# Key groups 4 to 7 transposed by DMA instead of by TensorE, with loads and transposes of the neighbouring turns moved, in a fused attention and MLP kernel

## The chip, the cores and the metric

The kernel runs on one core of a Trainium2 chip. The metric is the device time of one launch in microseconds. Three runs of the kernel before took 818.16, 818.71 and 819.41 us; the median, 818.71 us, is the time to compare with. Besides these there is one profiled execution, whose trace is read below.

## The reference, cut to what matters

```python
xn = layernorm(x)                                  # x: 2048 tokens x 576, bf16
# A: attention over the last 512 cached positions; 32 query heads, 16 key groups, head size 128
q = (xn @ wq).reshape(B, Sq, 32, 128).transpose(0, 2, 1, 3)
k = repeat(k_cache[:, :, Sk - 512:, :], 2, axis=1)
v = repeat(v_cache[:, :, Sk - 512:, :], 2, axis=1)
s = (softmax(q @ k.T * 128 ** -0.5) @ v).reshape(B, Sq, 4096) @ wo
# B: a token mixer (two 576x576 products with shifts by +-1 and +-2 tokens between), then an MLP of 4608
h = gelu(layernorm(xn) @ w1)
x1 = xn + shifted(h) @ w2
b = x1 + gelu(layernorm(x1) @ w3) @ w4
out = x + s * silu(b)
```

## The kernel before, in words

The 2048 tokens are worked in 4 query blocks of 512 (`QB`). The attention walks 128 **turns** `u`, one for each block and head (`u = 32*block + head`; in the code `Hq = 32`). In turn `u` TensorE computes the scores of head `u` (`stage_s`, L545: four 128x512 products with the transposed keys `kT`), the query projection of head `u+1` (`stage_q`, L526), and the value products of head `u-1` (`stage_v`, L564). ScalarE takes the exponentials (L549). VectorE copies the queries and divides by the row sums. The order is written out by hand for SP, POOL and PE in the loop at the end of the attention: for each turn the table `fill` gives side work that is put behind the first score products, `pe_fill` gives extra products for TensorE, and `turn` gives transposes that SP issues at the turn's end. The Tile scheduler orders VectorE and ScalarE.

Side work that the change touches:

- **Keys.** `load_k(i)` (L356) brings key groups 4i to 4i+3 into a staging tile of `stage_pool`, which has two buffers under one name. Loads 0 and 1 are issued by SP at the start, loads 2 and 3 by POOL in turns 4 and 12. Groups 0 to 3 are transposed by TensorE before turn 0. Groups 4 to 7 (`prep_k`, L372) are transposed by TensorE in turns 5, 7, 9 and 11, four 128x128 products each, into a PSUM tile that VectorE copies to `kT` (L376). Groups 8 to 15 are transposed by DMA (`tr_k`, L381), issued by SP in turns 9 to 12 and 17 to 20. Group g is first read in turn 2g.
- **Head outputs.** `stage_t(v)` (L577) transposes the output of head `v` by DMA from an `o` tile (18 buffers) into an `oT` tile (36 buffers). SP issues one per turn, none in the turns that have a `tr_k`, and two per turn after turn 37 until the backlog is gone.
- **Weights.** POOL loads `wq` for four heads in every fourth turn (`load_wq`, L339 and L346, two buffers): turns 3, 7, 11 and so on; load j is first read by `stage_q` in turn 4j-1, four turns after its issue. POOL loads `wo` in eight pieces of four heads (L412), in turns 9, 13, ... 37. Each waits with a small copy (L243) until that turn's exponentials are there. Values (L362) are loaded in turns 3 to 20, the next block's `x` (L332) in turn 14.
- **First output projection.** The product of block 0's heads with `wo` (`wo_groups`, L269) stands in turns 43 to 47 (`WO0 = 43`).
- **Mixer transposes.** `ln2_apply` (L209) and `tr2` (L260) normalise blocks 0 and 1 for the mixer and transpose them by DMA in turns 34 to 37 and 42 to 45 into two tiles of `stage_pool`, which is read only after the attention.
- **Mixer.** After the attention `b1_rest(b)` ends with a gelu on ScalarE (L847) and a DMA transpose (L848); the pairs (`b1_pair`, L812) have two gelus each. The list `aside` puts `b1_rest(3)` into step 3, ahead of the gelus of the pair of step 2.

SP and POOL are in-order queues: what waits holds up everything behind it.

Of the kernel before, what the change touches and what calls it, by code (L numbers as in the profile page):

```python
# [8 lines left out]
P = 128  # L9
ACT = mybir.ActivationFunctionType  # L10
ALU = mybir.AluOpType
AX = mybir.AxisListType
BF16 = mybir.dt.bfloat16
# [18 lines left out]
def kernel(  # L32
# [14 lines left out]
    nc = tc.nc  # L47
# [4 lines left out]
    _, Hkv, Sk, Dh = A_k_cache.shape  # L52
    assert Dh == P
    Hq = A_wq.shape[1] // Dh
# [7 lines left out]
    QB = 512  # L62
    NB = S // QB
    TB = QB // P
# [3 lines left out]
    NDC = NF + 1  # L68
    DP = NDC * P
    DCH = [(i * P, min(P, D - i * P)) for i in range(NDC)]  # L70
    M0 = 512
    R0 = D - M0
# [4 lines left out]
    OFF = 16  # L77
# [150 lines left out]
    oT_pool = octx.enter_context(tc.tile_pool(name="oT_pool", bufs=OT, side="right"))  # L228
    fence_pool = ctx.enter_context(tc.tile_pool(name="fence", bufs=2))
    tctx = ctx.enter_context(ExitStack())  # L230
    stage_pool = tctx.enter_context(tc.tile_pool(name="stage_pool", bufs=2))
    so_pool = tctx.enter_context(tc.tile_pool(name="so_pool", bufs=1))
    so_t, oT_t, xnnT = {}, {}, {}
    w1_all = xT_b[0][:].rearrange("p k q -> p (k q)")
# [16 lines left out]
                                in_=w1_tail.rearrange("p (j two s) -> p j two s", two=2, s=c4)[:, :, half, 0:P])  # L251
    flag_m = [None]

    def stage():
        return stage_pool.tile([P, DP * TB], BF16, name="stage")

    def tr2(b, tt, home=None):
        if tt == 0:
            xnnT[b] = (home or stage())[:].rearrange("p (k t) -> p k t", k=NDC)
        nc.sync.dma_start(out=xnnT[b][:, :, tt * P:(tt + 1) * P], in_=xm_b[b % 2][:, tt, :], transpose=True)  # L260

    FLAG_OPS = (ALU.max, ALU.min)
# [36 lines left out]
    with ExitStack() as actx:  # L299
# [5 lines left out]
        kT = res.tile([P, Hkv, W], BF16, name="kT")  # L305
        v_sb = res.tile([P, Hkv, KCH, VW], BF16, name="v_sb")
        NWQ = 2
        KDMA = 8
        PLAIN = 4
        wq_b = [res.tile([P, NDC, 4 * Dh], BF16, name=f"wq_b{i}") for i in range(NWQ)]  # L310
        ri_b = res.tile([P, Hq, TB], FP32, name="ri_b")
# [38 lines left out]
        kst_t = {}  # L350

        def load_k(i, eng=None, step=4):
            kst_t[i] = stage()
            dst = kst_t[i][:, 0:4 * W].rearrange("p (g a) -> p g a", g=4)
            for g in range(0, 4, step):
                (eng or nc.gpsimd).dma_start(  # L356
                    out=dst[:, g:g + step, :],
                    in_=A_k_cache[0, 4 * i + g:4 * i + g + step, K0:, :].rearrange("g (p kc) d -> p g (kc d)", p=P))
# [30 lines left out]
        for tt in range(TB):  # L389
            if tt:  # L390
                (nc.sync if tt < TB - 1 else nc.scalar).dma_start(out=x_first[:, tt, :],
                                                                  in_=x2[tt * P:(tt + 1) * P, :])
# [4 lines left out]
        with tc.manual_schedule(engines={SP}):  # L397
            load_k(0, nc.sync, 2)
            for m0 in (0, 2 * Dh):
                cols = slice(m0, m0 + 2 * Dh)  # L400
                nc.sync.dma_start(out=wq_b[0][:, 0:NF, cols],
                                  in_=A_wq[0:NF * P, cols].rearrange("(kc p) m -> p kc m", p=P))
# [220 lines left out]
            return PLAIN - 1 <= u < U - 1 and u % 4 == 3  # L623

        ln2_at = (7, Hq + 3, 2 * Hq - 4, 2 * Hq + 20)
        tr2_at = (Hq + 2, Hq + 10, 3 * Hq - 10, 3 * Hq - 5)
        WO0 = Hq + 11
        tr_k_at = {u: g for u, g in zip([*range(9, 13), *range(17, 21)], range(KDMA, Hkv))}
        x_at = (14, Hq + 12, 2 * Hq + 4)
        ln1_at = (19, Hq + 21, 2 * Hq + 16)  # L630

        for b in range(1, NB):
# [37 lines left out]
                pe_late.append((2 * g - 3, g))  # L670
        for j in range(2, NB * 8):
            at(4 * (j - 1) - 1, lambda j=j: load_wq(j))
        for i, u in enumerate((9, 13, 17, 21, 25, 29, 33, 37)):
            at(u, lambda i=i, u=u: late(pT_t[u][0][0:1, 0:1], lambda: load_wo(i)))
        for b in range(NB):
            at((b + 1) * Hq + 1, lambda b=b: row_range(b))
# [33 lines left out]
        for u in range(1, U + 1):  # L710
            n = 1
            if u in tr_k_at:
                turn[u] = [lambda g=tr_k_at[u]: tr_k(g)]
                n = 0
            elif u > Hq + 5:
                n = 2
            if u < WO0 + TB + 1:
                n = min(n, OT - done)
            for _ in range(min(n, u - done)):
                turn.setdefault(u, []).append(lambda v=done: stage_t(v))  # L720
                done += 1
# [28 lines left out]
    with ExitStack() as bctx:  # L750
# [23 lines left out]
        hq = mres.tile([P, HW], BF16, name="hq")  # L774
        hs = mres.tile([P, S], BF16, name="hs")
        h4 = [mres.tile([P, TB, P], BF16, name=f"h4_{i}") for i in range(NB)]
# [61 lines left out]
        def b1_rest(b):  # L838
            def ops(half, tt, k):
                w = w1_m[half, k, :].rearrange("p (g s) -> p g s", g=4)[:, :, P:c4] if k < NF else w1_q[half, :, :]  # L840
                return xnnT[b][half, k, tt * P:(tt + 1) * P], w

            pr = small_products(ops)
            gs = gs_pool.tile([P, TB, R0], FP32, name="gs")
            nc.vector.tensor_copy(out=gs[:], in_=pr[0])
            nc.vector.tensor_tensor(out=gs[:], in0=gs[:], in1=pr[1], op=ALU.add)
            nc.scalar.activation(out=h4[b][:, :, 0:R0], in_=gs[:], func=ACT.Gelu_apprx_tanh)  # L847
            nc.sync.dma_start(out=hq[:, OFF + b * QB:OFF + (b + 1) * QB].rearrange("p (t q) -> p t q", t=TB),  # L848
                              in_=h4[b][:].rearrange("p t c -> p (t c)"), transpose=True)

        def shifts(b):
            for g in (1, 0, 3, 2):
# [36 lines left out]
        with tc.manual_schedule(engines={SP, POOL, PE, DVE, ACTE}):  # L889
            for b in range(2, NB):  # L890
                home = mres.tile([P, DP * TB], BF16, name=f"xnnT{b}")
                for tt in range(TB):
                    tr2(b, tt, home)
            e = small.tile([P, 1], FP32, name="nr_e")
            nc.scalar.activation(out=e[:], in_=so_t[NB - 1][:, 1, 0:1], func=ACT.Gelu_apprx_tanh)
            for half in range(2):
                nc.gpsimd.dma_start(out=w1_q[HALVES[half], :, :],
                                    in_=w1_tail.rearrange("p (g s) -> p g s", g=4)[:, :, P:c4])
            for half in range(2):
                for g in range(4):  # L900
                    p0 = half * DR + g * rsz
                    nc.gpsimd.dma_start(out=w2_q[p0:p0 + rsz, :], in_=w2_by_g[g, P:c4, :])
            for t in (hb[:, :, OFF - PAD:OFF], hb[:, :, OFF + S:OFF + S + PAD], hq[:, OFF - PAD:OFF],
                      hq[:, OFF + S:OFF + S + PAD], *[t[:, :, R0:] for t in h4]):
                nc.gpsimd.memset(t, 0.0)
            nc.gpsimd.dma_start(out=mx_dram[:, :], in_=flag_m[0][:])
            nc.gpsimd.dma_start(out=m1[:], in_=mx_dram[:, :].rearrange("(o p) c -> o c p", o=1))
            ops = [(b1_pair, 0), (b1_pair, 1), (b2_pair, 0), (b1_pair, 2), (b2_pair, 1), (b1_pair, 3), (b2_pair, 2),
                   (b2_pair, 3)]
            ops = [(f, b, p) for f, b in ops for p in range(2)]  # L910
            aside = {0: [lambda: b1_rest(0)], 1: [lambda: b1_rest(1)], 2: [lambda: b1_rest(2)],
                     3: [lambda: b1_rest(3), lambda: shifts(0)], 6: [lambda: shifts(1)], 8: [lambda: shifts(2)],
                     10: [lambda: shifts(3)]}
            pend = None
            ln3_0 = ln3_steps(0)
            ln3_at = {7: 2, 8: 1, 11: 3, 12: 3}
            for k in range(len(ops) + 1):
                nxt = None
                if k < len(ops):
                    f, b, p = ops[k]  # L920
                    nxt = f(b, p, bank_pair((("pm0", "pm2"), ("pm1", "pm3"))[k % 3 - 1]) if k % 3 else h3_banks())
                    nxt[0]()
                for fn in aside.get(k, []):
                    fn()
                if pend:
                    pend[1]()
                    f, b, p = ops[k - 1]
                    if f is b2_pair and p == 1:
                        b2_rest(b)
                for _ in range(ln3_at.get(k, 0)):  # L930
                    ln3_0.pop(0)()
                pend = nxt
            while ln3_0:
                ln3_0.pop(0)()
            ln3_transpose(0)
            mm = small.tile([1, 2], FP32, name="mm", bufs=1)
            for k in range(2):
                nc.vector.tensor_reduce(out=mm[:, k:k + 1], in_=m1[:, k, :], axis=AX.X, op=FLAG_OPS[k])
            over = small.tile([1, 1], FP32, name="over", bufs=1)
            nc.vector.tensor_scalar(out=over[:], in0=mm[:, 0:1], scalar1=ROW_LIMIT, scalar2=None, op0=ALU.is_gt)  # L940
            nc.vector.scalar_tensor_tensor(out=flag_i[:], in0=mm[:, 1:2], scalar=1.0 / ROW_LIMIT, in1=over[:],
                                           op0=ALU.is_lt, op1=ALU.add)

            def wo_bank(shape, name):
                if name == "pswr":
                    return ps_h2.tile([P, QB], FP32, name="pr0")[:, 0:TB * R0].rearrange("p (t r) -> p t r", t=TB)
                return ps_h2.tile(shape, FP32, name="pr1" if wo_i else "pm0")

            wo_b = wo_groups(NB - 1, wo_bank, nc.scalar)
            for wo_i, i in enumerate((2, TB, 3)):  # L950
                for atom in wo_b[i]:
                    atom()
            nc.gpsimd.tensor_copy(out=gate[:, :], in_=hs[P // 2:P // 2 + 1, S - 1:S])
# [194 lines left out]
        with tc.manual_schedule(engines={PE, DVE, ACTE}):  # L1148
# [6 lines left out]
            g, j = 2, 0  # L1155
            for d in range(0, ND, 2):
                b = d // NP
# [3 lines left out]
                end = d % NP == NP - 2  # L1161
# [52 lines left out]
            b = NB - 1  # L1214
# [174 lines left out]
```

## Time and profile before

| | |
|---|---|
| median of 3 runs | 818.71 us (818.16 to 819.41) |
| the profiled execution's own time | 822.13 us |
| its span, first to last instruction | 820.6 us |
| mean granted TensorE clock | 0.996 |
| TensorE busy | 806.4 us (98%) |
| VectorE, ScalarE busy | 445.1, 445.7 us (54% each) |
| DMA, mean over the span | 98 GB/s |
| head turns, output products of the first block begin | 11 us, 137 us |
| mixer | from about 480 us |

The profiled execution took 3.4 us more than the median of the plain runs. Busy shares are over the whole span; TensorE is busy nearly everywhere, so what can be read is where its row of products has a gap, and which work it would no longer do. Times inside the trace count from the span's start.

### The profile page before, as it was taken

What the parts mean: (1) busy time and instruction counts of PE and PEld (TensorE: products, weight loads), DVE (VectorE), ACT (ScalarE), POOL (GpSimd) and SP (SyncE); (2) the same over time, 40 slices, a digit from 0 to 9 for tenths busy, and PEclk for the clock granted to TensorE, in tenths of its full rate; (3) what the DMA queues carried; (4) which work ended last, traced back from release to release, by engine and by line L of the source; (5) the groups of instructions that cost most, each with busy time, mean ns of one, the idle gap of its engine ahead of it and who ended that gap; (6) DMA issues with size and microseconds to landing.
All of it is one profiled execution on the core that took longest, in us unless ns stands there. A gap on an engine that the chain in (4) does not pass through costs nothing. (4 is left out here: it accounts for less than half of the span.)

```text
span 820.6 us, 19925 instructions
## 1 busy us (share of the span) xinstructions
PE 806.4 (98%) x8174; PEld 466.8 (57%) x8255; DVE 445.1 (54%) x1383; ACT 445.7 (54%) x798; POOL 125.2 (15%) x211
## 2 busy tenths in 40 slices
PE   8998999999999999999999999999999999999997
PEld 6664665566654656645666645655555555555555
DVE  6877686128831579722566528444246636655413
ACT  7887886248833788833788632033233423334620
POOL 3253221101101111100211211172000000000000
PEclk9999999999999999999999999999999999999999
DMA  8899996029821447520553472399000410320101
GB/s 212 143 204 195 171 190 137 29 66 143 156 67 42 91 105 135 110 49 14 107 130 101 79 99 63 66 324 282 3 2 16 77 59 16 48 88 16 45 15 38
DMA packets 135534, 80.73 MB, mean 98 GB/s; under 512 B 112112, under 2 KB 125712, under 8 KB 135440
## 3 DMA queue, kind: packets, MB, share of 16 engines
q1 hardware_dynamic: 121360, 39.32, 27.4%
q0 software_dynamic: 12832, 38.85, 18.6%
q8 instruction: 65, 1.06, 0.6%
q10 hardware_dynamic: 1248, 1.25, 0.5%
q14 instruction: 29, 0.24, 0.1%
HBM read 46.89 MB, written 6.93 MB: 66 GB/s over the span
## 5 line engine op out<-in xcount | busy, mean ns | idle before, releaser
L549 ACT ACTIVATE pT<-sc 128x512 bf16<-128x512 f32 x512 | 287.1, 599 | 96.4 <-PE sc L545 81.6
L545 PE MATMUL sc<-qT,kT 128*128 128x512 bf16 x504 | 167.6, 379 | 0.2
L564 PEld LDWEIGHTS <-pT 128*128 128x128 bf16 x2048 | 134.6, 98 | 53.2 <-issue 11.4
L564 PE MATMUL po<-v_sb,pT 128*128 128x129 bf16 x2048 | 158.3, 220 | 0.5
L526 PE MATMUL psq<-xT_b,wq_b 128*128 128x512 bf16 x455 | 123.2, 381 | 5.3 <-DMA wq_b<-in_A_wq_dram 2.5
L1022 PE MATMUL ph<-xT_b,w_s 64*128 64x512 bf16 x976 | 127.2, 376 | 0.0
L1059 PE MATMUL pm<-w_s,h 64*128 64x512 bf16 x864 | 122.0, 377 | 0.0
L1040 ACT ACTIVATE h<-ph 128x512 bf16<-128x512 f32 x67 | 39.4, 597 | 132.7 <-PE ph L1022 130.5
L569 DVE TENSOR_TENSOR o<-po,ri_b 128x256 bf16<-128x256 f32 x256 | 107.8, 421 | 6.3
L1059 PEld LDWEIGHTS <-h 64*128 64x128 bf16 x1728 | 70.2, 94 | 55.9
L269 PE MATMUL pswo<-wo_sb,oT 128*128 128x512 bf16 x434 | 101.2, 379 | 0.6
L269 PEld LDWEIGHTS <-oT 128*128 128x128 bf16 x1024 | 64.7, 98 | 54.2
L1059 PE MATMUL pr<-w_s,h 64*128 64x64 bf16 x864 | 89.6, 189 | 0.0
L536 DVE CAST qT<-psq 128x512 bf16<-128x512 f32 x64 | 44.0, 688 | 78.1 <-PE psq L511 45.4
L526 PEld LDWEIGHTS <-wq_b 128*128 128x128 bf16 x506 | 49.5, 98 | 61.2 <-DMA wq_b<-in_A_wq_dram 3.0
L1022 PEld LDWEIGHTS <-w_s 64*128 64x128 bf16 x1152 | 55.4, 94 | 49.0 <-issue 0.6
L534 DVE TENSOR_TENSOR qT<-psq,rq 128x512 bf16<-128x512 f32 x62 | 42.8, 690 | 65.1 <-ACT pT L549 57.9
L1038 DVE COPY hx<-ph 128x512 f32<-128x512 f32 x55 | 38.0, 692 | 60.7 <-PE ph L1022 60.7
L339 POOL DMA_DIRECT2D wq_b<-in_A_wq_dram x30 | 23.1, 770 | 272.1 <-PE sc L545 260.3
L568 DVE RECIPROCAL ri_b<-po 128x2 f32<-128x2 f32 x256 | 42.2, 165 | 37.8 <-PE po L564 32.9
L545 PEld LDWEIGHTS <-kT 128*128 128x128 bf16 x512 | 46.0, 98 | 21.1 <-DVE qT L534 0.4
L516 ACT ACTIVATE rq<-sc 128x512 f32<-128x512 f32 x62 | 33.6, 594 | 11.9 <-PE sc L511 11.9
(171 smaller groups left out, 702.1 us busy)
## 6 DMA issues: line engine op xcount, KB each, us to landing
wq_b<-in_A_wq_dram POOLq DMA_DIRECT2D x30, 512.0 KB, 5.2
wo_sb<-in_A_wo_dram POOLq DMA_DIRECT2D x8, 576.0 KB, 5.9
w_s<-in_B_w_dram POOLq DMA_DIRECT2D x9, 512.0 KB, 6.1
w_s<-in_B_w_dram POOLq DMA_DIRECT2D x10, 288.0 KB, 5.1
w_s<-in_B_w_dram POOLq DMA_DIRECT2D x4, 576.0 KB, 5.8
s_b<-s_dram SPq DMA_DIRECT2D x4, 576.0 KB, 5.4
x_b<-in_A_x_dram SPq DMA_DIRECT2D x4, 576.0 KB, 6.7
out_dram<-o SPq DMA_DIRECT2D x15, 144.0 KB, 1.8
```

Source lines behind the costliest of these rows:

```text
L269: nc.tensor.matmul(ps, lhsT=oT_t[qb * Hq + h][:, tt, :], rhs=wo_sb[:, h, lo:hi], start=(i == 0), stop=(i == Hq - 1))
L526: nc.tensor.matmul(psq[:, :], lhsT=w[:, kc, hh * Dh:(hh + 1) * Dh], rhs=xT_b[qb % 2][:, kc, :], start=(kc == 0 and not (two and hh == 1)), ...
L534: behind["qT"] = nc.vector.tensor_tensor(out=qT[:, :], in0=psq[:, :], in1=rq_t.pop(u)[:, :], op=ALU.add)
L536: nc.vector.tensor_copy(out=qT[:, :], in_=psq[:, :])
L545: nc.tensor.matmul(sc[:, :], lhsT=kT[:, g, kc * P:(kc + 1) * P], rhs=qT_t[u][:, :], start=True, stop=True)
L549: behind["exp"] = nc.scalar.activation(out=pT[:, :], in_=sc[:, :], func=ACT.Exp, scale=SCALE)
L564: nc.tensor.matmul(po[:, j, :], lhsT=pTs[kc][:, tt * P:(tt + 1) * P], rhs=v_sb[:, g, kc, 0:Dh + 1], start=(kc == 0), stop=(kc == KCH - 1))
L568: nc.vector.reciprocal(out=ri, in_=po[:, :, Dh])
L569: nc.vector.tensor_tensor(out=o[:, t0:t0 + 2, :], in0=po[:, :, 0:Dh], in1=ri.unsqueeze(2).to_broadcast([P, 2, Dh]), op=ALU.mult)
L1022: nc.tensor.matmul(ps[i][:, :], lhsT=lhsT, rhs=xT[half, kc, :], start=first, stop=last, skip_group_check=True)
L1040: nc.scalar.activation(out=h3[:, :], in_=src[:, :], func=ACT.Gelu_apprx_tanh)
L1059: nc.tensor.matmul(out, lhsT=h3_t[b, fc][half, tt * P:(tt + 1) * P], rhs=w4_s[fc // WS][half, fc % WS, lo:hi], start=key not in started, s ...
```

## The change

Groups 4 to 7 are transposed by DMA too: `KDMA` is 4 and `tr_k_at` has turns 3 to 6 as well. So TensorE's 16 transposes and VectorE's 4 copies are gone, and twelve turns in place of eight issue a key transpose instead of a head's. Two transposes per turn come only after turn 49. The staging tiles get two names with one buffer each. The eight `wo` loads stand in turns 13, 21, 25, 29, 33, 36, 38 and 41, the first output projection in turns 45 to 49, the load of block 2's `x` in turn 46, the mixer transposes in turns 67 to 70 and 71 to 74 with their `ln2_apply` in turns 65, 66, 69 and 70. In the mixer, gelu and transpose of `b1_rest(3)` follow the two gelus of the pair of step 2.

```diff
-    stage_pool = tctx.enter_context(tc.tile_pool(name="stage_pool", bufs=2))
+    stage_pool = tctx.enter_context(tc.tile_pool(name="stage_pool", bufs=1))
...
-    def stage():
-        return stage_pool.tile([P, DP * TB], BF16, name="stage")
+    def stage(i):
+        return stage_pool.tile([P, DP * TB], BF16, name=f"stage{i % 2}")
...
-            xnnT[b] = (home or stage())[:].rearrange("p (k t) -> p k t", k=NDC)
+            xnnT[b] = (home or stage(b))[:].rearrange("p (k t) -> p k t", k=NDC)
...
-        KDMA = 8
+        KDMA = 4
...
-            kst_t[i] = stage()
+            kst_t[i] = stage(i)
...
-        tr2_at = (Hq + 2, Hq + 10, 3 * Hq - 10, 3 * Hq - 5)
-        WO0 = Hq + 11
-        tr_k_at = {u: g for u, g in zip([*range(9, 13), *range(17, 21)], range(KDMA, Hkv))}
-        x_at = (14, Hq + 12, 2 * Hq + 4)
+        tr2_at = (2 * Hq + 3, 2 * Hq + 7, 3 * Hq - 10, 3 * Hq - 5)
+        WO0 = Hq + 13
+        tr_k_at = {u: g for u, g in zip([*range(3, 7), *range(9, 13), *range(17, 21)], range(KDMA, Hkv))}
+        x_at = (14, Hq + 14, 2 * Hq + 4)
...
-        for i, u in enumerate((9, 13, 17, 21, 25, 29, 33, 37)):
+        for i, u in enumerate((13, 21, 25, 29, 33, 36, 38, 41)):
...
-            elif u > Hq + 5:
+            elif u > WO0 + TB:
                 n = 2
...
-            nc.scalar.activation(out=h4[b][:, :, 0:R0], in_=gs[:], func=ACT.Gelu_apprx_tanh)
-            nc.sync.dma_start(out=hq[:, OFF + b * QB:OFF + (b + 1) * QB].rearrange("p (t q) -> p t q", t=TB),
-                              in_=h4[b][:].rearrange("p t c -> p (t c)"), transpose=True)
+
+            def end():
+                nc.scalar.activation(out=h4[b][:, :, 0:R0], in_=gs[:], func=ACT.Gelu_apprx_tanh)
+                nc.sync.dma_start(out=hq[:, OFF + b * QB:OFF + (b + 1) * QB].rearrange("p (t q) -> p t q", t=TB),
+                                  in_=h4[b][:].rearrange("p t c -> p (t c)"), transpose=True)
+
+            if b < NB - 1:
+                end()
+            return end
...
-                for fn in aside.get(k, []):
-                    fn()
+                ends = [fn() for fn in aside.get(k, [])]
                 if pend:
                     pend[1]()
+                    if k == 3:
+                        ends[0]()
```

How the order moves on SP's queue, from the last load of the start to turn 21 (`stage` and `stage_170` and so on are the staging tiles, `o` and `oT` a head's output before and after its transpose):

```order
-L356 DMA stage<-in_A_k_cache_dram 128x4x512
-L577 DMA_TRANSPOSE oT<-o 128x4x128 x8
-L381 DMA_TRANSPOSE kT<-stage 128x4x128 x4
+L356 DMA stage_170<-in_A_k_cache_dram 128x4x512
+L577 DMA_TRANSPOSE oT<-o 128x4x128 x2
+L381 DMA_TRANSPOSE kT<-stage_170 128x4x128 x4
+L577 DMA_TRANSPOSE oT<-o 128x4x128 x2
+L381 DMA_TRANSPOSE kT<-stage_512 128x4x128 x4
 L577 DMA_TRANSPOSE oT<-o 128x4x128 x4
-L381 DMA_TRANSPOSE kT<-stage 128x4x128 x4
+L381 DMA_TRANSPOSE kT<-stage_948 128x4x128 x4
 L577 DMA_TRANSPOSE oT<-o 128x4x128
```

Four key transposes stand ahead of the output of head 2; up to turn 21 SP issues 21 transposes as before, 12 of keys and 9 of heads where it was 8 and 13.

On POOL's queue, turns 7 to 13 (the `gate` copy is the wait for a turn's exponentials, `stage` the last key load):

```order
-L243 COPY gate<-pT 1x1
-L412 DMA wo_sb<-in_A_wo_dram 128x4x576
 L339 DMA wq_b_115<-in_A_wq_dram 128x4x512
 L346 DMA wq_b_115<-in_A_wq_dram 64x2x128 x2
-L356 DMA stage<-in_A_k_cache_dram 128x4x512
+L356 DMA stage_948<-in_A_k_cache_dram 128x4x512
 L362 DMA v_sb<-in_A_v_cache_dram 128x4x128 x2
 L243 COPY gate<-pT 1x1
```

The `wo` load of turn 9 is gone from here. The last key load keeps its place, but goes into the tile named `stage1`, whose last readers are the DMA transposes of groups 4 to 7.

On ScalarE in the mixer, of the changed kernel (`h_2` and `h_3` are the results of `b1_rest(2)` and `b1_rest(3)`, `hb` those of the pairs):

```order
L849 ACTIVATE h_2_8029<-gs 128x4x64
L812 ACTIVATE hb<-pm_8128 128x512
L812 ACTIVATE hb<-pm_8127 128x512
L812 ACTIVATE hb<-pm_8195 128x512
L812 ACTIVATE hb<-pm_8194 128x512
L849 ACTIVATE h_3_8030<-gs 128x4x64
L812 ACTIVATE hb<-ph_8262 128x512
```

Before, `h_3` stood between the second and the third `hb`.

## The prediction

> **What bounds the kernel now.** First the page's busy times, then the list of what TensorE waited for over the whole span (columns: who waited, for whom, us in total, times, longest).
>
> ```profile
> PE 806.4 (98%) x8174; PEld 466.8 (57%) x8255; DVE 445.1 (54%) x1383; ACT 445.7 (54%) x798; POOL 125.2 (15%) x211
> PE psq L526 <- DMA wq_b<-in_A_wq_dram: 2.5, 1, 2.5
> PE warm L683 <- POOL ident masks.py:199: 1.9, 1, 1.9
> PE warm L686 <- DVE nr_y L450: 0.4, 1, 0.4
> PE pm L786 <- ACT hb L812: 0.3, 1, 0.3
> ```
>
> TensorE sets the time, and its row of products is nearly closed. Only two gaps lie where the change works: one of 2.5 us for a `wq` load, and one of 0.3 us in the mixer. So an edit gains only by taking products from TensorE or by closing one of these gaps; relief for VectorE, ScalarE or a queue counts only through them.
>
> The timeline shows the first gap; the stretches around it (busy us of each engine, then granted clock, DMA share, GB/s) show what follows.
>
> ```profile
> 77.95 0.61 PE L526 MATMUL psq<-xT_b,wq_b 128*128 128x512 bf16 x1 [2.47 <-DMA wq_b<-in_A_wq_dram]
> ...
> 72.00:75.00 3.00, 3.00 (x30) 1.93 (x28) 2.90 (x17) 2.65 (x5) 0.96 (x2) 1.00 0.84 143
> 75.00:78.00 3.00, 0.53 (x4) 0.05 (x2) 2.08 (x11) 1.59 (x4) 0.61 (x1) 0.93 0.81 271
> 78.00:81.00 3.00, 2.78 (x10) 0.78 (x12) 0.59 (x1) 0.16 (x1) 0.60 (x1) 0.51 1.41 108
> 81.00:84.00 3.00, 3.00 (x33) 2.05 (x31) 2.60 (x10) 2.79 (x6) 0.00 (x0) 1.00 1.01 191
> ```
>
> After an idle time of 2.47 us the granted clock is 0.51 for 3 us, so the gap costs more than itself: 0.49 of 3 us is another 1.5 us, 4.0 us together. A second view gives the same. POOL issues one `wq` load every four turns, right after TensorE frees the buffer, so these issues are a clock of the turns:
>
> ```profile
> 28.36 0.75 POOL L339 DMA_DIRECT2D wq_b<-in_A_wq_dram  x1 [7.42 <-PE sc L545]
> 39.98 0.75 POOL L339 DMA_DIRECT2D wq_b<-in_A_wq_dram  x1 [2.07 <-PE sc L545]
> 47.92 0.78 POOL L356 DMA_DIRECT2D stage<-in_A_k_cache_dram  x1 [6.00 <-DMA kT<-stage]
> ...
> 62.56 0.75 POOL L339 DMA_DIRECT2D wq_b<-in_A_wq_dram  x1 [1.53 <-PE sc L545]
> 73.80 0.75 POOL L339 DMA_DIRECT2D wq_b<-in_A_wq_dram  x1 [1.59 <-PE sc L545]
> 88.99 0.75 POOL L339 DMA_DIRECT2D wq_b<-in_A_wq_dram  x1 [1.50 <-PE sc L545]
> 100.18 0.76 POOL L339 DMA_DIRECT2D wq_b<-in_A_wq_dram  x1 [0.53 <-PE sc L545]
> 111.34 0.75 POOL L339 DMA_DIRECT2D wq_b<-in_A_wq_dram  x1 [1.50 <-PE sc L545]
> ```
>
> Four undisturbed turns take 11.2 us (100.18 to 111.34); those with the gap take 15.2 (73.80 to 88.99): **4.0 us** more.
>
> Why is that load late? It is the one issued at 62.56, and 75.48 (77.95 less 2.47) is when TensorE wants it: a load has **12.9 us** from issue to use. The time to landing (least, median, largest us) of the loads issued at 62.56, 88.99 and 111.34, in this order:
>
> ```profile
> DMA to landing us min/median/max: 14.3/14.9/15.3
> DMA to landing us min/median/max: 7.3/7.7/8.0
> DMA to landing us min/median/max: 9.1/9.5/9.8
> ```
>
> Only the first misses 12.9. It has the DMA at its limit around it (share 1.09 over 60 to 80 us, below), and a jam before it: at 47.92 POOL had been held for 6.00 us by the last key load, which waited for transposes `kT<-stage`. Values, `wo`, `x` and the next `wq` stood behind and were then issued in one rush.
>
> ```profile
> 40.00:60.00 20.00, 19.79 (x181) 12.18 (x183) 15.54 (x53) 17.63 (x33) 11.03 (x19) 1.00 1.08 217
> 60.00:80.00 20.00, 17.21 (x145) 9.89 (x147) 14.82 (x57) 14.81 (x27) 7.09 (x11) 0.94 1.09 198
> 160.00:180.00 20.00, 19.89 (x210) 11.48 (x211) 3.67 (x10) 7.19 (x13) 1.95 (x3) 1.00 0.10 31
> ```
>
> **The change part by part. TensorE's transposes.** The first of the 16:
>
> ```profile
> 25.71 0.22 PE L372 MATMUL ps_k<-ident,stage 128*128 128x128 bf16 x1
> 25.77 0.38 PE L545 MATMUL sc<-qT,kT 128*128 128x512 bf16 x1
> L372 PE MATMUL ps_k<-ident,stage x16: 219/219/219, 25.7 to 44.5; 128*128 128x128 bf16 x16
> ```
>
> Each is modelled as 219 ns long, but the next product starts 0.06 us later. Sixteen at 0.06 are **0.9 us** (0.96, less the rounding of the starts). The turn clock agrees: 28.36 to 39.98 is 11.62, 0.45 over the undisturbed 11.2, with two groups in it. The upper bound would be 16 times 219 ns, 3.5 us. I take 0.9. The four VectorE copies gain nothing, since TensorE waits for none. The Trainium skill, "TensorE: Matmul & The Clock Gate", Part 4, has a transpose at about 275 ns within a kernel; by that the removal would be worth 4.4 us by estimate and the time 3.5 us lower than I forecast. The starts speak against that here.
>
> **The key transposes on SP.** The queue as it ran, and the key transposes' time to landing:
>
> ```profile
> 15.86 22.20 SPq L577 DMA_TRANSPOSE oT<-o  x8
> 38.16 6.32 SPq L381 DMA_TRANSPOSE kT<-stage  x4
> 44.58 5.16 SPq L577 DMA_TRANSPOSE oT<-o  x4
> 52.75 6.18 SPq L381 DMA_TRANSPOSE kT<-stage  x4
> 59.03 4.55 SPq L577 DMA_TRANSPOSE oT<-o  x1
> 76.84 1.20 SPq L461 DMA_TRANSPOSE xT_b<-xn_b  x1
> ...
> L381 SPq DMA_TRANSPOSE kT<-stage x8: 1192/1382/2206, 38.2 to 57.5; - x8
> DMA to landing us min/median/max: 4.2/8.5/13.7
> ```
>
> Heads 0 and 1 are issued by about 19 us (the first at 15.86, one per 2.8 us), then groups 4 to 7, 1.6 us apart (6.32 for four), from 20 to 26 us. Group 4 is first read in turn 8; turn 7's load is issued at 28.36 and that turn takes about 3, so it is wanted near 31.5. With the median landing of 8.5 us it is there at 28.5; groups 5 to 7 have about 5 us more each and follow 1.6 us apart. With the largest landing, 13.7, group 4 would be 2 us late and cost, at 4.0 us per 2.5 of gap, 3.3 us. I take nothing: in this stretch POOL has one `wq`, one key and one value load outstanding, not the jam at 55 us. Queued behind on SP are heads 2 and later, which nobody needs before the output product; that moves from turn 43 to 45, and its 36 `oT` tiles still fill before it. The heads in `o` tiles grow to 13 in turn 49, of 18 tiles: nothing as well, since SP then drains two per turn.
>
> **The POOL jam.** The last key load now follows the transposes of groups 4 to 7, done by about 35 us, so the 6.00 us wait should go and the loads of turns 12 to 15 start up to 6 us earlier, spread out. The `wo` pieces of turns 9 and 17 are gone from this stretch: two of 576 KB, at the 217 GB/s above 2.7 us each, 5.3 us of DMA time of which the late load needs 2.5. So that load should land about 5 us earlier, at 10 instead of 15 of its 12.9 us. The gap closes: **4.0 us** in the profiled execution.
>
> A rule speaks for a smaller price of the gap. The Trainium skill, "TensorE: Matmul & The Clock Gate", Part 1, has the clock halve only after an idle window of about 3.4 us; by that a gap of 2.47 us would cost itself alone, and closing it 2.5. The 0.51 above is against that reading here, so 4.0 stands.
>
> **What moves to later turns.** Five `wo` pieces now lie between turns 29 and 41, and the eight mixer transposes leave turns 34 to 45. Per four turns that is about as many `wo` bytes more as transposes less, so I take the 9.5 us landing of the load at 111.34 for these turns: within 12.9, nothing. The last piece, of turn 41, has over 11 us to turn 45. The mixer transposes go to turns 65 to 74, where the long output turns leave the DMA nearly idle (0.10 at 160 to 180 us, the same products of block 0): nothing.
>
> **The mixer.** ScalarE and TensorE there:
>
> ```profile
> 490.45 0.42 ACT L847 ACTIVATE h<-gs 128x256 bf16<-128x256 f32 x1 [1.43 <-DVE gs L846]
> 490.77 1.06 ACT L812 ACTIVATE hb<-pm 128x512 bf16<-128x512 f32 x2
> 491.88 1.47 PE L786 MATMUL pm<-xT_b,hb 64*128 64x512 bf16 x12 [0.28 <-ACT hb L812]
> ```
>
> ScalarE waited 1.43 us for VectorE with the pair's gelus behind it. With these first, they end over 0.3 us earlier and the 0.28 goes. The moved transpose lands some 0.7 us later; its reader comes several steps on. **0.3 us.**
>
> **The sum.** In the profiled execution 4.0 + 0.9 + 0.3 = 5.2 us: 820.6 becomes 815.4 of span, 822.13 becomes 816.9. But the plain runs' median lies 3.4 us under that execution. TensorE's row has no other gap that could hold so much, and the runs spread over 1.25 us, which a closed row of products wouldn't. So I read part of the 3.4 as a shorter gap in plain runs. It is then worth between 0.6 (4.0 less 3.4) and 4.0 there; I take 2.5, a little over the middle. The gain is 2.5 + 0.9 + 0.3 = 3.7, and the time **815.0 us**, with 813.5 to 816.9 from these two bounds.
>
> **The rivals.**
>
> The gap belongs to the profiled execution: only 0.6 + 0.9 + 0.3 = 1.8 us are left, 816.9. For it speaks the 3.4 us; against it that DMA is near its limit whatever is recorded.
>
> The change doesn't do what it should: one wait takes the place of the other. The last key load may still hold POOL, or group 4 or one `wq` load comes late by about 1.6 us and takes back 2.5: 817.5. For it speaks the DMA share of 1.08 from 40 us on, with 12 key transposes now ahead of the heads; against it the smaller load there.
>
> Slower, by one mechanism: more heads wait when SP comes free after the `xT_b` transposes (76.84 and later), 12 instead of 8, and SP issues them back to back from about 85 to 118 us beside `wq` and `wo`. Four `wq` loads lie in that stretch, with 7.7 and 9.5 us now, and they are late once they pass 12.9. Each us of lateness costs 1.6 (4.0 over 2.47). It decides from 5.3 / 1.6 = 3.3 us of lateness over the four together, where the gain of 3.7 is lost and 1.6 more; at 1.1 us each the price is 7.0 and the time 822.0. Against it: SP needs 1.3 us for each already, and with five heads in a row the loads still had 3 us in hand.
>
> TensorE's transposes cost their full 219 ns: 2.6 us more gain, 812.4. The starts are against it.
>
> **How the numbers follow.** The forecast has 0.60, the gap that belongs to the profile 0.14, the wait in its place 0.12, the slower case 0.12, the dearer transposes 0.02. A difference under 0.2% (1.6 us) can't be told from none here. Faster than 817.1: the forecast, the dear transposes and half of the first rival, 0.70; within 0.2%: the other half and the second rival, 0.18; slower 0.12. The range takes 813.0 to 818.0: both bounds of the gap and the second rival with some room, leaving out the slower and the dear-transpose case and a tail.
>
> **What would show it.** Right: no TensorE wait for `wq_b`; granted clock 1.00 from 60 to 84 us; every `wq` load 11.2 us after the one before, from 28 us on; no wait of POOL for `kT<-stage`; `wq` landings under 12.9 us; no `hb` wait in the mixer. Wrong: a TensorE wait for `kT` near 31 us, `wq` landings over 12.9 us between 85 and 130, a wait of L269 for `oT` or `wo_sb` in turn 45, or a median near 817 with a profile 5 us shorter, which would put the gap on the profile.

## The result, and the profile after

The changed kernel takes **823.1 us** (median of 14 runs, 821.62 to 828.1), the kernel before 818.67 us (14 runs, 817.67 to 823.66). The ratio is 1.0044 (1.0027 to 1.0062): 3.6 us slower (2.2 to 5.1). The forecast was 815.0 us, and even the top of its range, 818.0, is 3.6 us below the fastest run. The profiled execution took 823.11 us, with a span of 821.5. Of all runs below one is left out: one of the twelve of e9_store_act, at a granted clock of 0.556, took 1418.83 us.

From the page of the changed kernel, TensorE's busy time, and from its trace all that TensorE waited for over the whole span (who waited, for whom, us in total, times, longest):

```profile
PE 810.5 (99%) x8239; PEld 469.7 (57%) x8239; DVE 444.3 (54%) x1379; ACT 445.4 (54%) x798; POOL 125.2 (15%) x211
PE po L564 <- DVE o L569: 4.2, 1, 4.2
PE warm L683 <- POOL ident masks.py:199: 1.9, 1, 1.9
```

The wait for `wq_b` and the wait for `hb` are gone. One new wait stands there: 4.2 us for VectorE's division of a head's output.

**The early turns did what was forecast.** POOL's `wq` and key loads of the changed kernel, and the stretches in which the kernel before stood still (busy us of each engine, granted clock, DMA share, GB/s):

```profile
39.30 0.75 POOL L339 DMA_DIRECT2D wq_b<-in_A_wq_dram  x1 [7.72 <-PE sc L545]
41.23 0.79 POOL L356 DMA_DIRECT2D stage<-in_A_k_cache_dram  x1
61.65 0.75 POOL L339 DMA_DIRECT2D wq_b<-in_A_wq_dram  x1 [5.21 <-PE sc L545]
72.89 0.75 POOL L339 DMA_DIRECT2D wq_b<-in_A_wq_dram  x1 [1.58 <-PE sc L545]
84.07 0.75 POOL L339 DMA_DIRECT2D wq_b<-in_A_wq_dram  x1 [1.50 <-PE sc L545]
```

```profile
72.00:75.00 3.00, 3.00 (x27) 1.89 (x26) 2.86 (x16) 2.65 (x6) 1.94 (x3) 1.00 0.88 239
75.00:78.00 3.00, 3.00 (x29) 1.62 (x27) 2.96 (x13) 2.75 (x7) 0.00 (x0) 1.00 0.73 212
```

The key load no longer waits; four turns take 11.2 us (61.65 to 72.89 to 84.07; 39.30 to 61.65 is two times 11.2); TensorE is busy throughout at clock 1.00 where it idled for 2.47 us. The key transposes of the changed kernel, and their time to landing (least, median, largest):

```profile
L381 SPq DMA_TRANSPOSE kT<-stage x12: 1190/1276/3216, 20.0 to 53.3; - x12
DMA to landing us min/median/max: 4.3/6.6/9.9
```

None made TensorE wait. The load that had come late, now issued at 61.65, landed early:

```profile
DMA to landing us min/median/max: 3.3/3.5/4.0
```

And the mixer, where ScalarE now has the pair's gelus first:

```profile
490.95 1.09 ACT L812 ACTIVATE hb<-pm 128x512 bf16<-128x512 f32 x2 [0.89 <-PE pm L786]
491.92 0.42 ACT L849 ACTIVATE h<-gs 128x256 bf16<-128x256 f32 x1
```

**The loss is in one place.** The same clock of the turns later on, in the changed kernel:

```profile
269.78 0.76 POOL L339 DMA_DIRECT2D wq_b<-in_A_wq_dram  x1 [13.35 <-PE sc L545]
286.89 0.78 POOL L339 DMA_DIRECT2D wq_b<-in_A_wq_dram  x1 [15.15 <-PE sc L545]
```

The kernel before issued the load that stands here at 269.78 at 274.71, and the next at 285.88. So the changed kernel was 4.9 us ahead at that point, just what the forecast had for the profiled execution (4.0 and 0.9), and 1.0 us behind four turns later: 17.1 us in place of 11.2, **5.9 us lost**. What TensorE, VectorE and SP did there, in this order, each from the timeline of the changed kernel:

```profile
275.23 0.38 PE L545 MATMUL sc<-qT,kT 128*128 128x512 bf16 x1
279.81 1.05 PE L564 MATMUL po<-v_sb,pT 128*128 128x129 bf16 x8 [4.21 <-DVE o L569]
```

```profile
272.69 0.69 DVE L536 CAST qT<-psq 128x512 bf16<-128x512 f32 x1 [1.20 <-PE psq L511]
278.59 0.64 DVE L209 TENSOR_SCALAR xm_b<-xn_b,ln_mv,ln_r 128x576 bf16<-128x576 bf16 x2 [5.21 <-DMA stage<-xm_b]
279.14 0.16 DVE L568 RECIPROCAL ri_b<-po 128x2 f32<-128x2 f32 x1
279.33 0.42 DVE L569 TENSOR_TENSOR o<-po,ri_b 128x256 bf16<-128x256 f32 x1
```

```profile
259.05 1.27 SPq L260 DMA_TRANSPOSE stage<-xm_b  x1
269.00 0.38 SPq L284 DMA_DIRECT2D s_dram<-so  x1
269.48 1.57 SPq L577 DMA_TRANSPOSE oT<-o  x1
271.11 1.35 SPq L260 DMA_TRANSPOSE stage<-xm_b  x1
```

Read from TensorE backwards. It cannot write the next value product, because VectorE has not divided the last one out of its PSUM tile. VectorE's queue has a write of `xm_b` (`ln2_apply`, L209) ahead of that division, and the write waits 5.21 us for a DMA transpose that still reads the same tile. That is the fourth mixer transpose of block 0, issued by SP at 271.11 behind the store of the output product (269.00) and the transpose of a head (269.48). Its time to landing, beside that of the third (issued at 259.05), from the DMA view of each issue, the third first:

```profile
stage<-xm_b SPq DMA_TRANSPOSE x1, 2.6
...
stage<-xm_b SPq DMA_TRANSPOSE x1, 7.5
```

The windows show the price:

```profile
273.00:276.00 3.00, 2.61 (x24) 1.40 (x21) 0.38 (x1) 2.81 (x6) 0.00 (x0) 1.00 1.15 200
276.00:279.00 3.00, 0.00 (x0) 0.00 (x0) 0.41 (x2) 0.24 (x1) 0.00 (x0) 1.00 1.34 114
279.00:282.00 3.00, 2.19 (x18) 1.92 (x19) 2.41 (x9) 0.60 (x1) 0.00 (x0) 0.61 0.16 31
282.00:285.00 3.00, 3.00 (x24) 1.67 (x22) 1.50 (x5) 1.80 (x4) 0.00 (x0) 0.82 0.56 111
```

4.21 us of idle time, and then clocks of 0.61 and 0.82, which cost 0.39 and 0.18 of 3 us, 1.7 us: 5.9 in all, as the turn clock has it.

**Why a write of that tile stands there.** `xm_b` has two tiles, one for even blocks and one for odd ones. The code writes block 2's rows in turns 84 and 85, but VectorE's order is made by the scheduler, and it pulls these writes some 14 to 20 turns forward in both kernels. Before, nothing read the tile any more by then (the mixer transposes of block 0 were in turns 34 to 37), and the writes ran from 226 to 231 us without a wait. The first of them, from the timeline of the kernel before:

```profile
226.32 0.97 DVE L209 TENSOR_SCALAR xm_b<-xn_b,ln_mv,ln_r 128x576 bf16<-128x576 bf16 x3
```

The change moved the readers to turns 67 to 70 and left the writers to the scheduler, which put one behind each reader. VectorE's queue in the changed kernel, with what each row waits for (`xm_b_80` is the even tile, `xn_b_78` block 2's rows, DMAHW1 the DMA that still reads the tile):

```order
L536 COPY qT<-psq 128x512 [waits PE_49]
L209 TENSOR_SCALAR xm_b_80<-xn_b_78,ln_mv_84,ln_r_88 128x576 [waits DMAHW1_49]
L209 TENSOR_SCALAR xm_b_80<-xn_b_78,ln_mv_84,ln_r_88 128x64
L568 RECIPROCAL ri_b<-po 128x2 [waits PE_49]
L569 TENSOR_TENSOR o<-po,ri_b 128x256 [waits DVE_49]
```

There are four such pairs, each with a wait for a DMA. VectorE waited 17.3 us in them; the first three (at 242, 252 and 262 us, about 4 us each) cost TensorE nothing, since they fall in turns of the output product, which are some 10 us long and give TensorE other work. The fourth falls in a short turn after it: the last product of `wo` ends at 268.4 us. The Trainium skill, "TensorE: Matmul & The Clock Gate", Part 1, calls VectorE's queue strictly first in, first out; the trace agrees: the product that the division at 279.14 reads was done by 274.1 us, and the division ran only after the write.

### The profile page after: what moved, and what is told of

It is laid out like the page before. It is cut to its first block, busy times and chain, and to the rows that moved or that the text cites. A ratio compares the mean times of both kernels' runs of the same rounds, so it can differ in the third digit from the quotient of the medians.

```text
span 821.5 us, 19964 instructions
## 1 busy us (share of the span) xinstructions
PE 810.5 (99%) x8239; PEld 469.7 (57%) x8239; DVE 444.3 (54%) x1379; ACT 445.4 (54%) x798; POOL 125.2 (15%) x211
## 3 DMA queue, kind: packets, MB, share of 16 engines
q10 hardware_dynamic: 1248, 1.25, 0.5%
## 5 line engine op out<-in xcount | busy, mean ns | idle before, releaser
L545 PE MATMUL sc<-qT,kT 128*128 128x512 bf16 x512 | 171.0, 381 | 0.0
L526 PE MATMUL psq<-xT_b,wq_b 128*128 128x512 bf16 x506 | 129.9, 379 | 0.0
L269 PE MATMUL pswo<-wo_sb,oT 128*128 128x512 bf16 x448 | 103.2, 379 | 0.0
L1047 ACT ACTIVATE h<-hx 128x512 bf16<-128x512 f32 x55 | 34.6, 630 | 6.2 <-DVE hx L1045 2.0
```

The source lines that it names most:

```text
L269: nc.tensor.matmul(ps, lhsT=oT_t[qb * Hq + h][:, tt, :], rhs=wo_sb[:, h, lo:hi], start=(i == 0), stop=(i == Hq - 1))
L526: nc.tensor.matmul(psq[:, :], lhsT=w[:, kc, hh * Dh:(hh + 1) * Dh], rhs=xT_b[qb % 2][:, kc, :], start=(kc == 0 and not (two and hh == 1)), ...
L545: nc.tensor.matmul(sc[:, :], lhsT=kT[:, g, kc * P:(kc + 1) * P], rhs=qT_t[u][:, :], start=True, stop=True)
L1047: nc.scalar.activation(out=h3[:, :], in_=src[:, :], func=ACT.Gelu_apprx_tanh)
```

## The experiments

The theory: the whole loss is VectorE's wait for the moved mixer transposes. Rivals: the key transposes or the later `wo` pieces cost something too, or the store on SP ahead of the fourth transpose is the real cause. The first four kernels ran beside 31 runs of the kernel before (median 819.56 us, 817.67 to 825.34), the next four beside 23 (819.43, 817.59 to 824.95), the last beside 16 (819.49, 817.42 to 824.89).

### e1_held: the change, with block 2's writes held in their turn

```diff
+        def held(b, tt):
+            with tc.issue_after(behind["qT"].ins) if b == 2 else ExitStack():
+                ln2_apply(b, tt)
...
-                at(tr2_at[b] - 2 + tt // 2, lambda b=b, tt=tt: ln2_apply(b, tt))
+                at(tr2_at[b] - 2 + tt // 2, lambda b=b, tt=tt: held(b, tt))
```

> The changed kernel, with one difference: block 2's four ln2_apply writes of xm_b are put in VectorE's queue behind the query copy of their own turns 84 and 85, instead of where the scheduler had hoisted them (turns 66 to 71). The moved mixer transposes stay in turns 67 to 74. Theory A (VectorE's in-order queue: those hoisted writes wait for the moved transposes that still read xm_b, the fourth of which stands behind the store of the output product on SP, and the head outputs wait behind them): TensorE's 4.21 us gap at 275.6 us goes, and with it about 1.7 us at half clock; the profile's span falls from 821.5 to about 815.6, and the plain time from 823.1 to about 817.2, 1.5 under the kernel before. Rival B (the loss comes from the early turns, the twelve key transposes and the DMA load, and the gap only takes up slack): the time stays at 821 or above.

Measured: 817.27 us (12 runs, 816.83 to 819.86), 0.9965 of the time before (0.9947 to 0.9983). Block 2's writes ran at 308 to 322 us, VectorE waited for none of them and TensorE for no division. Against the change that is 5.8 us by the medians, and the trace lost 5.9 there; by the two ratios it is 0.79%, 6.5 us, whose intervals take in both. So the early writes make the loss, and the change without them is faster than before. In its profiled execution another gap came up:

```profile
66.18 0.39 PE L526 MATMUL psq<-xT_b,wq_b 128*128 128x512 bf16 x1 [2.92 <-DMA wq_b<-in_A_wq_dram]
```

```profile
wq_b<-in_A_wq_dram POOLq DMA_DIRECT2D x1, 512.0 KB, 13.2
```

It is a `wq` load again, but the one of turn 15, issued at 52.89 and wanted at 63.26 (66.18 less 2.92). It has only 10.4 us in hand, not 12.9, since POOL issues it late, and it took 13.2; in the changed kernel's profile the same load took 7.3. So e1_held takes the loss away with the mixer transposes and the store where the change has them.

### e2_mixer_back: the change, with block 0's and block 1's mixer transposes where they were

```diff
-        tr2_at = (2 * Hq + 3, 2 * Hq + 7, 3 * Hq - 10, 3 * Hq - 5)
+        tr2_at = (Hq + 2, Hq + 10, 3 * Hq - 10, 3 * Hq - 5)
```

> The changed kernel with the mixer transposes of blocks 0 and 1 back in turns 34 to 37 and 42 to 45 (ln2_apply two turns ahead of each), all else as changed. Theory A: no VectorE wait for a transpose, the gap at 275.6 us goes, about 817.2 us as with the held writes; if the eight transposes crowd the wo loads of turns 33 to 41, a TensorE wait for wq_b appears near 110 to 130 us and the time is 1 to 4 us higher. Rival B: 821 or above.

Measured: 817.69 us (12 runs, 816.96 to 820.28), 0.9961 (0.9939 to 0.9983). The writes ran near 225 us as before, without a wait. What TensorE waited for, of all that lies in the attention:

```profile
PE psq L526 <- DMA wq_b<-in_A_wq_dram: 2.5, 1, 2.5
```

That is the load of turn 15 once more. The key transposes, the `wo` turns and the later output product, all still in this kernel, cost nothing that shows.

### e3_mixer_only: the kernel before, with the mixer transposes alone moved

```diff
-        tr2_at = (Hq + 2, Hq + 10, 3 * Hq - 10, 3 * Hq - 5)
+        tr2_at = (2 * Hq + 3, 2 * Hq + 7, 3 * Hq - 10, 3 * Hq - 5)
```

> The kernel before with one edit: the mixer transposes of blocks 0 and 1 in turns 67 to 74 and their ln2_apply two turns ahead; keys, weights and output product as before. Theory A: this edit alone makes the loss: a TensorE gap of about 4 us near 281 us, 5.9 us in all, so about 824.6 us plain; the profile keeps the gap of the kernel before at 75 us too. Rival B: no such gap, 818.7 us.

Measured: 825.91 us (8 runs, 822.55 to 828.48), 1.0072 (1.0043 to 1.0102), so 5.9 us slower (3.5 to 8.4). TensorE's wait, and the clock of the turns:

```profile
PE po L564 <- DVE o L569: 3.5, 1, 3.5
```

```profile
270.61 0.76 POOL L339 DMA_DIRECT2D wq_b<-in_A_wq_dram  x1 [13.34 <-PE sc L545]
287.11 0.79 POOL L339 DMA_DIRECT2D wq_b<-in_A_wq_dram  x1 [14.54 <-PE sc L545]
```

16.5 us in place of 11.2, 5.3 lost in the same turn. This one line of the change makes the loss alone. This execution had no `wq` gap, though its early turns are those of the kernel before.

### e4_keys_only: the kernel before, with the key transposes by DMA and the named buffers alone

Beside the lines of the named buffers, which stand at e6_names_only:

```diff
-        KDMA = 8
+        KDMA = 4
...
-        tr_k_at = {u: g for u, g in zip([*range(9, 13), *range(17, 21)], range(KDMA, Hkv))}
+        tr_k_at = {u: g for u, g in zip([*range(3, 7), *range(9, 13), *range(17, 21)], range(KDMA, Hkv))}
```

> The kernel before with groups 4 to 7 transposed by DMA in turns 3 to 6 and the two named staging tiles; wo loads, output product, mixer transposes and mixer as before. Theory A says nothing is lost here: 0.9 us for the 16 products off TensorE, and in the profile the 75 us gap smaller or gone, since the last key load no longer holds POOL for 6 us: profile span 815.7 to 819.7. In plain runs 0.9 plus what that gap costs there; if it is mostly of the profiled execution (0.5 us in plain runs, from the changed kernel's 0.9 us in the profile against 4.4 in plain runs), 817.3; if it is there in full, 813.8. Rival B: slower than before, 820 or more.

Measured: 817.67 us (12 runs, 817.14 to 819.93), 0.9967 (0.9945 to 0.9990): 2.7 us faster (0.8 to 4.5). The last key load was issued without a wait, and no `wq` gap was in the profile:

```profile
41.44 0.79 POOL L356 DMA_DIRECT2D stage<-in_A_k_cache_dram  x1
```

So, within these intervals, nearly all of the gain lies in this part; the `wo` pieces that were taken out of the early turns are not needed for it.

### e5_packed: the change, with block 0's four mixer transposes together in turn 67

```diff
-                    at(tr2_at[b] + tt, lambda b=b, tt=tt: tr2(b, tt))
+                    at(tr2_at[b] + (tt if b else 0), lambda b=b, tt=tt: tr2(b, tt))
```

> The changed kernel with block 0's four mixer transposes all in turn 67, ahead of the store, instead of one each in turns 67 to 70; VectorE's early writes of xm_b stay where they are. Theory A, sharpened (the early writes cost only where the transpose they wait for is issued behind the store on SP and the wait falls into short turns, not because they wait at all): VectorE waits only in the long output turn 67, TensorE has no gap, about 817.2 us. If any such wait costs, a TensorE gap of 1 to 4 us appears in turn 67 or 68, near 235 to 245 us, and the time is 818.5 to 823.

Measured: 817.01 us (12 runs, 816.56 to 818.95), 0.9964 (0.9943 to 0.9985). VectorE's four waits are still there, but all in one long turn, the first and the last of them:

```profile
242.03 0.64 DVE L209 TENSOR_SCALAR xm_b<-xn_b,ln_mv,ln_r 128x576 bf16<-128x576 bf16 x2 [3.95 <-DMA stage<-xm_b]
...
246.01 0.64 DVE L209 TENSOR_SCALAR xm_b<-xn_b,ln_mv,ln_r 128x576 bf16<-128x576 bf16 x2 [0.68 <-DMA stage<-xm_b]
```

TensorE waited for none of them. The waits are shorter here too (6.0 us together, where the change had 17.3), so this run alone does not part place from length. The change itself does: its first three waits, up to 4.17 us long, cost nothing under an output product, and the fourth, outside one, cost 5.9 us. The place decides, not the presence.

### e6_names_only: the kernel before, with the two named staging buffers alone

```diff
-    stage_pool = tctx.enter_context(tc.tile_pool(name="stage_pool", bufs=2))
+    stage_pool = tctx.enter_context(tc.tile_pool(name="stage_pool", bufs=1))
...
-        return stage_pool.tile([P, DP * TB], BF16, name="stage")
+        return stage_pool.tile([P, DP * TB], BF16, name=f"stage{i % 2}")
```

> The kernel before with the two named staging tiles alone. The last key load should no longer wait 6.0 us for the DMA transposes of groups 8 to 11, since its tile was last read by TensorE in turn 11: POOL's wait before L356 falls from 6.0 us to under 3, and the wq load of turn 15 is issued near 53 us instead of 53.9. TensorE's 16 transposes stay, so a run without a wq gap takes about 818.1 us.

Measured, one execution: 818.66 us, span 817.1. The last key load:

```profile
45.03 0.78 POOL L356 DMA_DIRECT2D stage<-in_A_k_cache_dram  x1 [3.12 <-PE sc L545]
```

It waits 3.12 us for TensorE's score products and no longer 6.00 us for `kT<-stage`. But the `wq` load of turn 15 was issued at 53.88 all the same, as before, and the gap shrank to 0.5 us:

```profile
PE psq L526 <- DMA wq_b<-in_A_wq_dram: 0.5, 1, 0.5
```

So the hold of POOL alone did not set when that load starts, against what the forecast had taken. One execution cannot say whether the names made the gap smaller, since the next experiment shows that the gap changes from one execution to the next.

### e7_before_again: the kernel before, unchanged, profiled again

> The kernel before, unchanged, looked at once more. If its 2.47 us gap for wq_b is a matter of the single execution, as the spread of its plain runs suggests (about half near 818, a third at 822 to 825), this profile may have no gap, with about 818.1 us of its own time and the late load (issued near 62.5 us) landing in under 12.9 us; if the gap belongs to every profiled execution, it is there again with about 822.

Measured, one execution: 821.37 us, span 819.8. The gap came at another load, and what followed:

```profile
65.93 1.04 PE L526 MATMUL psq<-xT_b,wq_b 128*128 128x512 bf16 x3 [2.01 <-DMA wq_b<-in_A_wq_dram]
```

```profile
66.00:69.00 3.00, 2.95 (x16) 1.45 (x18) 1.42 (x3) 1.08 (x2) 2.12 (x3) 0.66 1.16 226
69.00:72.00 3.00, 3.00 (x22) 1.85 (x20) 2.47 (x10) 1.74 (x5) 0.00 (x0) 0.77 1.34 257
```

The late load is that of turn 15 here. The one after it again took 13.9 us, but the turns had been put back by then, and it was in time. POOL was held longer here as well: the last key load waited 7.67 us, not 6.00, and this load was issued at 54.65, not 53.88. So the kernel before has two loads on the edge, and which is late changes from one execution to the next.

### e8_best: the writes held, and the first `wo` piece in turn 17 in place of 13

As e1_held, and

```diff
-        for i, u in enumerate((13, 21, 25, 29, 33, 36, 38, 41)):
+        for i, u in enumerate((17, 21, 25, 29, 33, 36, 38, 41)):
```

> The changed kernel with block 2's writes held to their own turns and the first wo piece in turn 17 instead of 13, so that less stands ahead of the wq load of turn 15, which was late in the profiles of the first two experiments (landing 13.2 and 12.8 us). No VectorE wait for a transpose, that load landing in under 10 us, no TensorE gap: median about 817.0 us and no run above 818.5. If the late load has another cause, runs of 819 to 820 stay.

Measured: 816.99 us (12 runs, 816.62 to 817.62), 0.9958 (0.9940 to 0.9976), 3.4 us faster than before (2.0 to 4.9). The load of turn 15 landed after 6.7 us, and no execution was over 817.62, where e1_held had three over 818. The median is within 0.3 us of e1_held's. What the moved piece seems to take away is the tail; twelve runs each, in two batches, do not settle that, since the same load had landed after 7.3 us in the change too, with the piece still in turn 13.

### e9_store_act: the change, with all stores of the output product on ScalarE's queue

```diff
-            return wo_groups(qb, bank, nc.scalar if last else nc.sync)
+            return wo_groups(qb, bank, nc.scalar)
```

> The changed kernel with the stores of the output product (L284) issued by ScalarE instead of SP, so that SP isn't held by the store of turn 69. VectorE's early writes and the mixer transposes' turns stay; the scheduler puts the fourth early write a turn earlier. Theory A, about the place: the fourth transpose came 10 us after the third only because the store stood ahead of it on SP (270.4 would be 261 to 267 without). Then it is issued by about 267 us and landed by 270, VectorE's wait ends there, TensorE's gap shrinks from 4.21 to under 1 us and the time is 817 to 818.5. If the early write costs as soon as it waits in the last output turn, store or not, a gap of 2 us or more stays and the time is 820 or more.

Measured: 819.0 us (median of 11 runs, 818.77 to 822.89), 0.9994 (0.9969 to 1.0018), no difference from before, and between the two times that were forecast. TensorE's wait, SP's queue and VectorE's wait:

```profile
PE po L564 <- DVE o L569: 1.7, 1, 1.7
```

```profile
258.86 1.27 SPq L260 DMA_TRANSPOSE stage<-xm_b  x1
267.34 1.19 SPq L577 DMA_TRANSPOSE oT<-o  x1
268.58 1.27 SPq L260 DMA_TRANSPOSE stage<-xm_b  x1
```

```profile
273.31 0.43 DVE L209 TENSOR_SCALAR xm_b<-xn_b,ln_mv,ln_r 128x576 bf16<-128x576 bf16 x1 [3.22 <-DMA stage<-xm_b]
```

Without the store ahead of it the fourth transpose starts 2.5 us earlier (268.58, not 271.11) and lands after 4.7 us, not 7.5. It still comes 9.7 us after the third (it was 12.1), since it stands a turn later, behind the transpose of a head at 267.34; the expectation that it came late only because of the store did not hold. The gap shrinks from 4.21 to 1.73 us, without a fall of the clock: 1.8 us lost in place of 5.9. But the scheduler also put the fourth write a turn earlier here, so how much of the 4.1 us is the store's is not shown. What is shown is that the loss does not need the store: VectorE's wait of 3.22 us, outside the output product, still costs TensorE 1.73, and in e1_held nothing is lost with the store in place.

## Why the prediction was wrong

**The step that failed** is the one on what moves to later turns: "The mixer transposes go to turns 65 to 74, where the long output turns leave the DMA nearly idle …: nothing." It asked whether the transposes would find the DMA free and whether `wq` would suffer. It did not ask who writes the tile that they read. That next writer was on VectorE, right behind each reader; its wait for the fourth cost 5.9 us of TensorE's time, where the forecast had nothing. It showed in the order of VectorE's queue; the working had followed SP, POOL and ScalarE only, since the diff moves nothing on VectorE by hand. e1_held, e2_mixer_back and e5_packed take the loss away in three ways, and e3_mixer_only makes it alone: this is shown. "Nearly idle" failed as well at the place itself: the DMA share is 1.15 and 1.34 from 273 to 279 us, with the transpose of a head on each side of the fourth mixer transpose, and that one took 7.5 us to land where the third took 2.6. The place was misread, too: the output product of block 1 fills turns 65 to 69, so the transposes of turns 70 to 74, the fourth among them, have no long turn to stand in.

The other steps held, the jam in part:

- TensorE's transposes, 0.9: the changed kernel is 4.9 us ahead at 269.78, which is 0.9 and the 4.0 of the gap. Ahead of the gap it leads by 0.9 already (52.97, not 53.88). The dearer price of 3.5 would have put it 7.5 ahead.
- The POOL jam: the wait of the key load is gone, and so is the gap in this execution; the load in question, issued at 61.65, landed after 4.0 us at most, where the forecast had 10. But the load of turn 15, which was to start up to 6 us earlier, started 0.9 earlier (52.97, not 53.88), only as much as the turns had gained. So the stretch was not eased by earlier `wq` starts; less in flight may have done it, which is not shown (e4_keys_only keeps the `wo` pieces and had no gap either). And the load of turn 15 has 10.4 us in hand, not the 12.9 that the forecast took for every load; it stayed on the edge, as e1_held and e2_mixer_back show.
- The key transposes on SP, nothing: no wait for `kT`, landings of at most 9.9 us against a bound of 13.7.
- The mixer, 0.3: the wait for `hb` is gone.
- What TensorE lost to one gap: 4.21 us of idle time cost 5.9, by the way of reckoning that the forecast used for 2.47 and 4.0.

**A second term, probably too large,** is the `wq` gap in plain runs. The forecast took 2.5 us off the median of 818.71, from bounds of 0.6 and 4.0. The runs of before reach down to 817.42 to 817.67 in each set, and their medians lie 1.0 (14 runs) to 2.1 us (16 runs) above that; the best kernels reach 816.56 to 816.83, about 1.0 lower than the lowest before, close to the 0.9 and 0.3 of the other terms. So the gap seems to be worth 1 to 2 us on the median, and what the ratios leave after 1.2 says the same: 1.7 in e1_held and 2.2 in e8_best, each by 1.5 us either way, so that 2.5 is not ruled out. The forecast also took the spread of 1.25 us as a sign of a gap; e8_best, whose profile has none, spreads over 1.0. The gap belongs neither to the profiled execution, as the first rival had it, nor to every run: of 31 runs of before, 12 are above 821.8. That reading rests on the spread of the runs and two profiles with the gap; what decides in one execution whether a load lands in 10 or in 15 us stays open. With the failed step mended, the time is 817.0 to 817.7 (e1_held, e2_mixer_back, e5_packed, e8_best), in the range, but near the first rival's 816.9 and not at 815.0; the rival meets the number by luck, since it had the gap in the profiled execution alone. The span of 815.4 forecast for the profiled execution is what e5_packed has.

The **rivals**: a wait did take the place of the one removed, but on another engine, at another place and at more than twice the price that was given to it (5.9, not 2.5). The slower case had the right side and the wrong mechanism: SP's back-to-back transposes from 85 us on made no `wq` load late. The load issued at 84.07 in the changed kernel, with the largest landing of that stretch:

```profile
DMA to landing us min/median/max: 9.5/9.7/10.0
```

That leaves 2.9 of the 12.9 us. The chance of 0.12 for slower held this one mechanism, on the queues that the diff names. None of the signs that were to show it wrong was a wait of VectorE.

## What to carry to other kernels

When a change moves the reader of a reused buffer, find that buffer's next writer in the built order of its engine, not in the source, and ask what stands behind the writer: a scheduler may have pulled it far ahead, and an in-order queue turns it into a stop for everything else. Read the built order of every engine with its waits, those that the diff does not touch too. And before a gap from one profiled execution goes into a sum, compare the lowest and the median of the plain runs: here their distance, 1.0 to 2.1 us, came nearer to what closing the gap brought than the 4.0 of the profile.

## What the runs showed of the hardware

The clock does not follow the length of a gap alone. It fell after idle times of TensorE of 2.01 us (e7_before_again, rows above), 2.47 (before), 3.54 (e3_mixer_only, to 0.65 and 0.78 for 3 us each) and 4.21 us (the change); it stayed at 1.00 after 1.73 (e9_store_act) and 2.52 (e2_mixer_back), and after 2.92 us in e1_held:

```profile
66.00:69.00 3.00, 2.76 (x25) 1.54 (x27) 1.42 (x4) 1.21 (x3) 1.53 (x2) 1.00 0.57 168
```

So a gap of 2 us cost 3.8 us of turn clock in e7_before_again (62.23 to 77.27, less 11.2), and one of 2.9 us in e1_held little more than itself (61.57 to 75.91, less 11.2, is 3.1). The Trainium skill, "TensorE: Matmul & The Clock Gate", Part 1, has the clock fall after an idle window of about 3.4 us that runs freely, so by that rule only the gaps of 3.54 and 4.21 us could have brought it down. That it fell after these agrees; that it fell after 2.01 and 2.47 us, shorter than the window, does not. Why it fell after these and not after 2.52 and 2.92 us stays open.
